# A Fourier layer and two expert layers on one core: ScalarE's order in the expert steps, and eight more conversion turns in the transform

## The chip, the cores and the metric

The kernel runs as one program on one core of a Trainium2 chip. The metric is the device time of that program in microseconds (us). Three runs of the kernel before gave 1172.59, 1174.08 and 1174.28 us; the median is 1174.08 us.

## The reference

Three layers follow each other on 2 x 3008 tokens of 256 numbers:

```
X = rfft(x, axis=1);  Yr = Xr @ w_r - Xi @ w_i + b_r;  Yi = Xr @ w_i + Xi @ w_r + b_i
Y = sign(Y) * max(|Y| - 0.01, 0)          # on the real and the imaginary part
x1 = irfft(Y, n=3008)                      # 6016 x 256
h = x1 @ w_in;  x2 = (h * cos(h)) @ w_out  # w_in 256 x 2048, w_out 2048 x 256
h = x2 @ w_in2; out = (h * clip(h + 3, 0, 6) / 6) @ w_out2
```

The expert weights arrive as float64 and are turned into float32 on the core.

## The kernel before, in words

**Two float32r pieces.** Each operand of a matmul is split into a high part (a copy on ScalarE) and a low part (a subtraction on GpSimd or VectorE), and a product is three matmuls (`three`, L844).

**Transform.** The Fourier layer runs in 24 steps (`k2_step`, L711), one for each pair of frequencies of one batch: w products (`w_mm`, PSUM tile pp), their split (`w_split`, tiles ph), the second transform stage (`b_mm`, bp), the shrinkage (`shrink_a` on ScalarE, `shrink_b` on VectorE, `shrink_hi` on ScalarE, `shrink_lo` on VectorE, which writes sl), the first inverse stage (`v_mm`, vp) and its store to DRAM (`v_store`, u_dram). The last inverse stage works on 16 groups of columns with two slices each (`y_mm`, PSUM tile yp; `y_out` copies it out on ScalarE, to st or yo). Groups 0, 1 and 2 follow steps 15, 16 and 17 (L785); their operands u_sb and tg_sb are loaded by `load_u`, the first one after step 14 (L783), each next one by `y_out` of the second slice. Three transform blocks and the other 26 slices run in the expert part.

**Expert steps.** The loop at L966 has 96 steps k (48 for each expert layer; 8 to each block of tokens). A step computes seven products of a fast 2 x 2 block scheme in four PSUM banks a, b, c, d (tiles ha to hd); bank a is always bank 0. Each of the four results then goes through `first` (ScalarE, then VectorE), `second` (Sin on ScalarE and a VectorE product, first layer alone) and `split` (gh on ScalarE, gl on GpSimd), and is multiplied with w_out some steps later (`out_mm`, six matmuls, tile acc). In each of the steps 1 to 12 two slices of the inverse transform are done as well, both in bank 0: the first by `y_begin(); y_end()` (L1025), the second by `y_begin()` at L1030 and `y_end()` at L1036. So the second slice waits for the copy yo of the first one, and block a of the next step waits for the copy yo of the second one. `advance` (L931) takes one step further in building the tokens of the next block (tile tok: a copy on ScalarE, subtractions on GpSimd); in steps 4 to 7 it does so three times a step.

**Conversion turns.** `Converter` (L281) turns the float64 weights into float32 pieces beside all that. Its work is cut into turns; `cv.step(n)` does n of them. A chunk of weights (128 x 512) is loaded by SP (rawi, rawo), its magnitude is taken on ScalarE (`magnitude`, L200: one ACTIVATE, tiles cvai and cvao), and then five turns do `clamp`, `shift`, `top`, `exponent`, `rest`, one VectorE instruction each (L203, L206, L209, L212, L215); `rest` hands an addition to GpSimd, and every second chunk of w_in has two more turns of sums on GpSimd. While a chunk is in its five turns, the pieces of the chunk before it are cut on ScalarE (L275), subtracted on GpSimd (L173) and stored by SP (L255). The magnitude of the next chunk is put on a list by `rest` and is done at the next `catch_up()`: at the start of each turn (L350), twice in a transform step (L734, L739) and once in an expert step (L1022).

`RATE_W` (L49) gives the turns of a transform step at its three places, for steps 0 to 7, 8 to 15, 16 to 20, and 21 to 23. An expert step has turns at three places (`other`, L939): one before `ba.first()`, and up to step 5 two before `bd.first()` and two at the end; in steps 8 to 47 the middle place has none.

**What sets the order.** In the transform the orders of TensorE, ScalarE and SP are those of the program; VectorE and GpSimd are ordered by a planner, which starts a conversion instruction early when its operands are there. In the expert steps all five orders are those of the program. Each engine and SP's queue take their instructions in order, so one that waits holds up those behind it.

Of the kernel before, what the change touches and what calls it, by code (L numbers as in the profile page):

```python
# [45 lines left out]


LASTC = 20
RATE_W = ((2, 1, 2), (1, 0, 1), (1, 1, 1), (0, 0, 0))  # L49
XB = 3  # L50
STAGED = [0] * 9 + [1, 2, 4, 5, 7, 8, 10] + [12] * 10
Y_EARLY = range(15, 18)
# [71 lines left out]
def fourier_moe_moe_kernel(ctx, tc, x, w_r, w_i, b_r, b_i, ta, tg, fg, win1, wout1, win2, wout2, out):  # L124
# [42 lines left out]
    def pool_now():  # L167
        while later:
            op, tiles = later.pop(0)
            op(*tiles)  # L170
# [110 lines left out]
    class Converter:  # L281
# [10 lines left out]
        def add(self, m, cs):  # L292
            for c in cs:
                self.queue += [("i", m, c, 0), ("i", m, c, 1), ("o", m, c, 0), ("o", m, c, 1)]
            while len(self.loaded) < 2 - self.busy and self.queue:
                self.load()
# [14 lines left out]
        def chunk(self):  # L311
            first = self.prev[0][0] if self.prev else None
            tail = self.tail()
            if self.loaded:
                key, ops = self.loaded.pop(0)
                self.busy = 1
                if not self.begun:
                    for _ in range(3):
                        next(tail, None)
                        yield  # L320
                    ops["magnitude"]()
                for part in ("clamp", "shift", "top", "exponent", "rest"):
                    if first == "i" or part in ("top", "exponent", "rest"):
                        next(tail, None)
                    if part == "rest":
                        for _ in tail:
                            pass
                        pool_now()
                    ops[part]()
                    if part == "rest":  # L330
                        if self.loaded:
                            self.ahead.append(self.loaded[0][1]["magnitude"])
                    yield
                self.begun = bool(self.loaded)
                yield from ops["sums"]()
                if ops["split"]:
                    self.prev = (key, ops)
                self.busy = 0
                self.load()
            else:  # L340
                yield from tail
# [5 lines left out]
        def step(self, n):  # L347
            for _ in range(n):
                pool_now()
                self.catch_up()  # L350
                while next(self.course, "end") == "end":
                    if not self.loaded and not self.prev:
                        return
                    if self.prev and self.prev[0] == self.hold:
                        return
                    self.course = self.chunk()
# [6 lines left out]
    cv = Converter()  # L363
# [33 lines left out]
    def y_out(g, ec):  # L397
        yp, at = yp_t.pop((g, ec)), g * YT
        if 0 not in staged:
            staged[0] = persist.tile([128, 2, 2, 512], F32, tag="st", bufs=1, name="st0")  # L400
        for t in range(2):
            t0, t1 = max(at, t * HALF[0]), min(at + YT, (t + 1) * HALF[0])
            if t0 < t1:
                act.activation(staged[0][:, ec, t, t0 - t * HALF[0] : t1 - t * HALF[0]], yp[:, t0 - at : t1 - at], AF.Copy)
        first = max(STARTS[1] - at, 0)
        if first < YT:
            yo = persist.tile([128, 512], F32, tag="o", bufs=3, name=f"yo{g}_{ec}")
            act.activation(yo[:, first:YT], yp[:, first:YT], AF.Copy)  # L408
        if ec == 1:
            load_u(g + 1)  # L410
        for p in range(1, NJ):
            t0, t1 = max(at, STARTS[p]), min(at + YT, STARTS[p + 1])
            if t0 < t1:
                sp.dma_start(x_dram[0][p][ec, :, t0 - STARTS[p] : t1 - STARTS[p]], yo[:, t0 - at : t1 - at])
# [69 lines left out]
    with ExitStack() as actx:  # L484
        apool = actx.enter_context(tc.tile_pool(name="apool", bufs=1))
        with tc.manual_schedule(engines={mybir.EngineType.PE, mybir.EngineType.SP, mybir.EngineType.Activation}):
# [224 lines left out]
            def k2_step(i):  # L711
                now, late, last = (divmod(i - k, NP) for k in range(1, 4))
                b, p = divmod(i, NP)
                rate = RATE_W[i // 8 + (i > LASTC)]
                more = i < NB * NP
# [85 lines left out]
    with tc.manual_schedule(engines=engines):  # L801
# [39 lines left out]
        def bank(z, name):  # L841
            return psum.tile([128, 512], F32, tag=f"h{z}", bufs=1, name=name)

        def three(h, ws, xs, start, stop, n):  # L844
            for j, (w, x) in enumerate(((ws[0], xs[0]), (ws[0], xs[1]), (ws[1], xs[0]))):
                pe.matmul(h[:, :n], lhsT=w, rhs=x, start=start and j == 0, stop=stop and j == 2, skip_group_check=True)  # L846

        def weights(k, slot):
            m, q = k // G, k % STEPS
            w, i = wi_sb[m, q // 2], q % 2  # L850
            return [w[:, z, slot - SLOTS[m][0], i * 128 : (i + 1) * 128] for z in range(2)]

        def tokens(k, slot):
            jj = k // STEPS
            return [tok[jj][:, z, slot - SLOTS[k // G][0], : HALF[jj % NJ]] for z in range(2)]
# [66 lines left out]
        def prepare(k):  # L922
            nonlocal ready
            jj, q = divmod(k, STEPS)
            if jj + 1 == 2 * NJ:
                return
            if q == (1 if jj else 3):
                stage_in(jj + 1)
                ready = operands(jj + 1)

        def advance(k, spare):  # L931
            if k % STEPS > (1 if k >= STEPS else 3) and not (spare and k >= STEPS):
                next(ready, None)

        def drained(k):
            if k < 2 and pend:
                pend.pop(0)()
# [13 lines left out]
        def y_end():  # L951
            if y_open:
                y_out(*y_open.pop())
# [4 lines left out]
        def flush():  # L958
            while ended:
                finish(*ended.pop(0))  # L960

        def out_next(least=1):
            if len(waiting) >= least:
                out_mm(waiting.pop(0))

        for k in range(2 * G):  # L966
            n = HALF[k // STEPS % NJ]
            a, b, c, d = (bank(z, f"h{r}_{k}") for z, r in zip((0, 1, 2, 3) if k % 2 == 0 else (0, 3, 2, 1), "abcd"))
            ba, bd, be, bc = (Block(k, f, t, h) for f, t, h in ((0, 0, a), (0, 1, d), (1, 0, b), (1, 1, c)))

            def mm(h, w, x, start=False):
                three(h, weights(k, w), tokens(k, x), start, True, n)

            if k == 0:
                for h in (b, d):
                    pe.matmul(h, lhsT=weights(k, A11)[0], rhs=tokens(k, B11)[0], start=True, stop=True)
            mm(a, A11, B11, True)
            act.activation(b[:, :n], a[:, :n], AF.Copy)  # L978
            if old:
                od, oe, oc = old  # L980
                od.split()
                oe.second()
            drained(k)
            out_next(5)
            mm(c, S1, T1, True)
            p5 = persist.tile([128, 512], F32, tag="r", bufs=5, name=f"p5_{k}")
            act.activation(p5[:, :n], c[:, :n], AF.Copy)  # L987
            if old:
                oc.split()
            drained(k)  # L990
            mm(b, S2, T2)
            add(d, p5, b, n)
            if k == 0:
                drained(k)
                next(ready)
            flush()
            mm(a, A12, B21)
            if old:
                oe.split()
            prepare(k)  # L1000
            advance(k, False)
            defer[0] = 2
            other(k, 0)
            defer[0] = 1
            ba.first()
            if k == 0:
                drained(k)
            out_next()
            pool_now()
            mm(b, S3, T3)  # L1010
            add(c, p5, b, n)
            ba.second()
            if k == 0:
                next(ready, None)
            mm(d, S4, B22)
            if k == 0:
                drained(k)
            other(k, 1)
            bd.first()
            advance(k, True)  # L1020
            bc.first()
            cv.catch_up()  # L1022
            out_next()
            if k:
                y_begin()  # L1025
                y_end()
            bd.second()
            mm(b, A22, T4)
            if k:
                y_begin()  # L1030
            else:
                drained(k)
            be.first()
            advance(k, False)
            bc.second()
            y_end()  # L1036
            out_next()
            other(k, 2)
            ba.split()
            flush()  # L1040
            old = bd, be, bc
            waiting += [ba, bd, be, bc]
            w_loads(k)
# [50 lines left out]
```

## Time and profile before

| | |
|---|---|
| median of three runs | 1174.08 us |
| profiled execution: its own time | 1174.28 us |
| its span, first to last instruction | 1172.5 us |
| TensorE busy | 1153.6 us (98%) |
| VectorE, ScalarE, GpSimd busy | 767.0, 811.3, 807.6 us |
| granted TensorE clock, mean | 0.998 |

Matmuls overlap, so busy time is a union of their spans, and short holes between two starts can hide in it. A wait of TensorE is best read from the timeline: the idle time in brackets, and the distance of two starts.

### The profile page before, as it was taken

What the parts mean: (1) busy time and instruction counts of PE and PEld (TensorE: products, weight loads), DVE (VectorE), ACT (ScalarE), POOL (GpSimd) and SP (SyncE); (2) the same over time, 40 slices, a digit from 0 to 9 for tenths busy, and PEclk for the clock granted to TensorE, in tenths of its full rate; (3) what the DMA queues carried; (4) which work ended last, traced back from release to release, by engine and by line L of the source; (5) the groups of instructions that cost most, each with busy time, mean ns of one, the idle gap of its engine ahead of it and who ended that gap; (6) DMA issues with size and microseconds to landing.
All of it is one profiled execution on the core that took longest, in us unless ns stands there. A gap on an engine that the chain in (4) does not pass through costs nothing.

```text
span 1172.5 us, 15903 instructions
## 1 busy us (share of the span) xinstructions
PE 1153.6 (98%) x5363; PEld 966.2 (82%) x5363; DVE 767.0 (65%) x1098; ACT 811.3 (69%) x1546; POOL 807.6 (69%) x654
## 2 busy tenths in 40 slices
PE   8999999999999999999999999999999999999998
PEld 7887877778888888888889987888888888888897
DVE  5888778786679888988897677643343444433442
ACT  4677677777788888888788875565566556556554
POOL 3566536896787797888887786557757667577544
PEclk9999999999999999999999999999999999999999
DMA  8646639635413113104115420020020010100000
GB/s 214 183 124 180 180 88 292 218 100 163 144 54 104 41 59 131 37 18 149 36 37 180 182 93 1 1 72 1 1 72 1 19 54 1 67 1 1 37 1 32
DMA packets 48106, 98.71 MB, mean 84 GB/s; under 512 B 6228, under 2 KB 22840, under 8 KB 47384
## 3 DMA queue, kind: packets, MB, share of 16 engines
q1 hardware_dynamic: 47768, 97.54, 26.2%
q8 instruction: 42, 0.69, 0.2%
q14 instruction: 40, 0.33, 0.1%
q10 hardware_dynamic: 256, 0.15, 0.0%
HBM read 59.53 MB, written 38.14 MB: 83 GB/s over the span
## 4 chain that ended last, share of the span: by engine, by line
PE 88%; DMA 3%; DVE 3%; ACT 2%; issue 2%; POOL 2%; POOLq 0%; ACTq 0%; SPq 0%; DVEq 0%
PE acc L846 41%; PE hb L846 15%; PE ha L846 11%; PE hc L846 5%; PE hd L846 5%; PE pp L633 4%; PE bp L660 2%; PE yp L389 2%; PE zp L528 1%; POOL gl L173 1%; PE vp L699 1%; DMA ta_big<-in_ta_dram 1%; DMA x_big<-in_x_dram 1%; DVE r L822 0%; DMA tg_sb<-in_tg_dram 0%
## 5 line engine op out<-in xcount | busy, mean ns | idle before, releaser
L173 POOL TENSOR_TENSOR gl<-r,gh 128x512 fp32r<-128x512 f32 (+1 forms) x384 | 501.3, 1321 | 280.7 <-ACT gh L837 264.4
L846 PE MATMUL acc<-gh,wo 128*128 128x512 f32 (+1 forms) x1536 | 529.6, 386 | 0.0
L846 PEld LDWEIGHTS acc<-gh,wo 128*128 128x128 f32 x1536 | 288.4, 188 | 53.5
L846 PE MATMUL acc<-gl,wo 128*128 128x512 f32 (+1 forms) x768 | 296.0, 385 | 0.6 <-POOL gl L173 0.6
L846 PE MATMUL hb<-tok,wi 128*128 128x512 f32 (+1 forms) x864 | 241.0, 387 | 0.6 <-DVE hc L858 0.6
L837 ACT ACTIVATE gh<-r 128x512 fp32r<-128x512 f32 (+1 forms) x384 | 227.6, 615 | 0.4 <-PE acc L846 0.4
L846 PEld LDWEIGHTS hb<-tok,wi 128*128 128x128 f32 x864 | 161.0, 188 | 31.1 <-DVE hc L858 2.0
L858 DVE TENSOR_TENSOR hd<-p,hb 128x512 f32<-128x512 f32 (+1 forms) x96 | 65.8, 685 | 164.1 <-PE hb L846 159.1
L846 PEld LDWEIGHTS acc<-gl,wo 128*128 128x128 f32 x768 | 144.2, 188 | 27.6 <-POOL gl L173 1.0
L846 PE MATMUL ha<-tok,wi 128*128 128x512 f32 (+1 forms) x576 | 160.5, 387 | 2.5 <-ACT yo L408 2.5
L830 ACT ACTIVATE r<-r 128x512 f32<-128x512 f32 (+1 forms) x192 | 118.9, 619 | 57.9 <-DVE r L822 57.9
L846 PEld LDWEIGHTS ha<-tok,wi 128*128 128x128 f32 x576 | 107.5, 188 | 24.8 <-ACT yo L408 5.1
L447 POOL TENSOR_TENSOR tok<-st,tok 128x512 fp32r<-128x512 f32 (+1 forms) x77 | 97.6, 1283 | 2.9 <-ACT tok L444 2.9
L987 ACT ACTIVATE p<-hc 128x512 f32<-128x512 f32 (+1 forms) x96 | 56.5, 588 | 58.2 <-PE hc L846 58.2
L824 ACT ACTIVATE r<-hd 128x512 f32<-128x512 f32 (+1 forms) x48 | 28.3, 589 | 78.1 <-PE hd L846 78.1
L846 PE MATMUL hc<-tok,wi 128*128 128x512 f32 (+1 forms) x288 | 80.2, 387 | 1.1 <-DVE r L831 1.1
L978 ACT ACTIVATE hb<-ha 128x512 f32<-128x512 f32 (+1 forms) x96 | 55.2, 575 | 37.7 <-PE ha L846 37.5
L846 PE MATMUL hd<-tok,wi 128*128 128x512 f32 (+1 forms) x288 | 79.7, 385 | 0.0
L858 DVE TENSOR_TENSOR hc<-p,hb 128x512 f32<-128x512 f32 (+1 forms) x96 | 65.4, 681 | 15.7 <-PE hb L846 14.9
L846 PEld LDWEIGHTS hc<-tok,wi 128*128 128x128 f32 x288 | 53.8, 188 | 12.5 <-DVE r L831 2.6
L846 PEld LDWEIGHTS hd<-tok,wi 128*128 128x128 f32 x288 | 54.1, 188 | 10.1
L450 POOL TENSOR_TENSOR st<-st 128x512 f32<-128x512 f32 (+1 forms) x44 | 57.9, 1317 | 1.2
(141 smaller groups left out, 1681.0 us busy)
## 6 DMA issues: line engine op xcount, KB each, us to landing
st<-x_dram SPq DMA_DIRECT2D x18, 512.0 KB, 4.7
wi<-wi_dram SPq DMA_DIRECT2D x5, 1792.0 KB, 8.3
rawi<-in_win_dram SPq DMA_DIRECT2D x16, 512.0 KB, 3.9
rawo<-in_wout_dram SPq DMA_DIRECT2D x16, 512.0 KB, 4.0
u_dram<-v SPq DMA_DIRECT2D x48, 128.0 KB, 2.4
u_sb<-u_dram SPq DMA_DIRECT2D x16, 384.0 KB, 3.9
wo<-wo_dram SPq DMA_DIRECT2D x10, 512.0 KB, 6.9
x_dram<-o SPq DMA_DIRECT2D x20, 256.0 KB, 2.2
```

The source lines that it names most:

```text
L173: nc.gpsimd.tensor_tensor(out, x, y, op=ALU.subtract)
L389: pe.matmul(yp[:, i * TP : (i + 1) * TP], lhsT=u_sb[g][:, i, ec * 128 : (ec + 1) * 128], rhs=tg_sb[g][:, i * TP : (i + 1) * TP], start=Tru ...
L447: subtract(at(lo, t), src, f32(at(hi, t)), op=ALU.subtract)
L450: subtract(z, x, y, op=ALU.subtract)
L633: pe.matmul(pp.rearrange("p a e -> p (a e)"), lhsT=za[:, p, kc, 2 * (k2 % 2) : 2 * (k2 % 2) + 2, :].rearrange("p r n -> p (r n)"), rhs=wb[ ...
L824: act.activation(r, h, AF.Relu, bias=3.0, scale=1.0)
L830: act.activation(r, r, AF.Sin, bias=math.pi / 2, scale=1.0)
L837: act.activation(gh[:, :n], self.r[:, :n], AF.Copy)
L846: pe.matmul(h[:, :n], lhsT=w, rhs=x, start=start and j == 0, stop=stop and j == 2, skip_group_check=True)
L858: dve.tensor_tensor(h[:, :n], r[:, :n], x[:, :n], op=ALU.add)
L978: act.activation(b[:, :n], a[:, :n], AF.Copy)
L987: act.activation(p5[:, :n], c[:, :n], AF.Copy)
```

## The change

Four edits:

1. `RATE_W`: one turn at the middle place of transform steps 8 to 15, where there was none: eight more turns in all, so that every later turn comes earlier, until the converter stops at its hold.
2. The start of a turn no longer catches up; a magnitude still on the list is done by the `clamp` turn, behind the piece that this turn cuts.
3. In the expert step `catch_up()` moves from behind `bc.first()` to behind `bc.second()`.
4. `y_end()` of the second slice moves ahead of `advance(k, False)` and `bc.second()`, directly behind `be.first()`.

```diff
-RATE_W = ((2, 1, 2), (1, 0, 1), (1, 1, 1), (0, 0, 0))
+RATE_W = ((2, 1, 2), (1, 1, 1), (1, 1, 1), (0, 0, 0))
...
-                    if part == "rest":
+                    if part == "clamp":
+                        self.catch_up()
+                    elif part == "rest":
                         for _ in tail:
                             pass
                         pool_now()
...
                 pool_now()
-                self.catch_up()
                 while next(self.course, "end") == "end":
...
             bc.first()
-            cv.catch_up()
             out_next()
             if k:
                 y_begin()
...
             be.first()
+            y_end()
             advance(k, False)
             bc.second()
-            y_end()
+            cv.catch_up()
             out_next()
```

## Rows read from the trace of the kernel before

**Rows 1.** The page: busy us (share) xinstructions.

```profile
PE 1153.6 (98%) x5363; PEld 966.2 (82%) x5363; DVE 767.0 (65%) x1098; ACT 811.3 (69%) x1546; POOL 807.6 (69%) x654
```

**Rows 2.** Waits of PE, whole span: line waited for, us in total, times, longest.

```profile
PE ha L846 <- ACT yo L408: 2.5, 4, 1.3
PE yp L389 <- ACT yo L408: 1.5, 4, 0.5
PE vp L699 <- DVE sl L693: 1.3, 2, 1.0
PE yp L389 <- DVE r L831: 0.9, 2, 0.4
```

**Rows 3.** Stretches: length, busy PE (x) PEld DVE ACT POOL, PEclk, DMA, GB/s.

```profile
77.00:117.00 40.00, 38.38 (x175) 31.69 (x174) 33.20 (x46) 31.58 (x61) 27.83 (x22) 1.00 0.59 173
116.70:120.10 3.40, 3.40 (x15) 3.02 (x14) 3.30 (x6) 1.46 (x3) 1.12 (x2) 0.50 0.40 116
183.00:305.00 122.00, 117.45 (x581) 95.24 (x580) 93.17 (x130) 93.81 (x181) 90.42 (x73) 1.00 0.56 178
305.00:1148.00 843.00, 842.39 (x3790) 707.94 (x3790) 526.60 (x748) 587.34 (x1111) 611.14 (x483) 1.00 0.16 54
```

**Rows 4.** Timeline of PE: start us, us, instruction [idle before <-releaser]; waits of transform and steps.

```profile
115.71 2.83 PE L389 MATMUL yp<-tg_sb,u_sb 96*128 96x94 f32 x16 [1.62 <-DMA tg_sb<-in_tg_dram]
130.58 0.69 PE L389 MATMUL yp<-tg_sb,u_sb 96*128 96x94 f32 x5
...
148.05 0.39 PE L699 MATMUL vp<-sh,fgr 128*128 128x512 f32 x1
149.47 0.50 PE L699 MATMUL vp<-sl,fgr 128*128 128x512 f32 x1 [1.03 <-DVE sl L693]
...
185.37 1.13 PE L389 MATMUL yp<-tg_sb,u_sb 96*128 96x94 f32 x8 [0.37 <-ACT yo L408]
188.14 0.96 PE L846 MATMUL ha<-tok,wi 128*128 128x512 f32 x3 [0.23 <-ACT yo L408]
...
227.57 0.97 PE L846 MATMUL ha<-tok,wi 128*128 128x512 f32 x3 [0.73 <-ACT yo L408]
241.32 0.96 PE L846 MATMUL ha<-tok,wi 128*128 128x512 f32 x3 [1.32 <-ACT yo L408]
```

**Rows 5.** Timeline of ACT, expert steps 1 and 5: same columns.

```profile
183.29 0.70 ACT L200 ACTIVATE cvai<-rawi 128x512 f32<-128x512 f32 x1 [1.17 <-POOL whio020l L173]
...
238.49 0.58 ACT L821 ACTIVATE r<-hb 128x512 int32<-128x512 f32 x1
239.75 0.63 ACT L444 ACTIVATE tok<-st 128x512 fp32r<-128x512 f32 x1 [0.68 <-POOL st L450]
240.28 0.61 ACT L830 ACTIVATE r<-r 128x512 f32<-128x512 f32 x1
240.80 0.46 ACT L408 ACTIVATE yo<-yp 128x376 f32<-128x376 f32 x1
```

**Rows 6.** Timeline of DVE in transform steps 10 and 20, same columns.

```profile
89.16 0.42 DVE L203 TENSOR_SCALAR cvao<-cvao 128x512 f32<-128x512 f32 x1
...
143.23 1.28 DVE L203 TENSOR_SCALAR cvao<-cvao 128x512 f32<-128x512 f32 x1
144.54 1.40 DVE L206 TENSOR_SCALAR cvao<-cvao 128x512 uint32<-128x512 uint32 x1
145.86 0.68 DVE L683 SCALAR_TENSOR_TENSOR u<-bp,u 128x512 f32<-128x512 f32 x1
147.66 1.76 DVE L693 TENSOR_TENSOR sl<-u,sh 128x512 fp32r<-128x512 f32 x1
```

**Rows 7.** Timeline of POOL beside the second row of rows 6, same columns.

```profile
142.94 1.29 POOL L447 TENSOR_TENSOR tok<-st,tok 128x512 fp32r<-128x512 f32 x1
```

**Rows 8.** Timeline of SP's queue (issue of DMAs), same columns.

```profile
126.35 0.37 SPq L380 DMA_DIRECT2D tg_sb<-in_tg_dram  x1
```

**Rows 9.** The page's DMA issues: KB each, median us from issue to landing.

```profile
u_sb<-u_dram SPq DMA_DIRECT2D x16, 384.0 KB, 3.9
```

## The prediction

> **What bounds the kernel now.** I read the page first: TensorE is busy 1153.6 of 1172.5 us, and no other engine reaches 70% [rows 1]. Then the stretches: from 305 to 1148 us TensorE is busy 842.39 of 843 us, and its 3790 matmuls come one every 0.22 us [rows 3]. Nothing can be won there, and something is lost only where another engine would become late by whole microseconds. So the time is the matmuls plus the holes ahead of 305 us and at the two ends, and the third view is TensorE's own waits [rows 2]. Of these the change can touch four kinds: block a of the next step waits for the copy yo of the second slice (2.5 us, 4 times), a slice waits for yo of the one before (1.5 us, 4 times, one of them in the drain) or for VectorE to free bank 0 (0.9 us, twice), and v_mm waits for sl (1.3 us, twice). The largest single hole, 1.62 us at 115.71, is the first slice of group 0 waiting for its load [rows 4], and behind it the clock is granted at 0.50, which is 1.2 of 2.4 GHz, for 3.4 us [rows 3].
>
> A wait costs more than its idle time shows, because the pipeline has to fill again: at 149.47 the idle time is 1.03 us, but the two starts lie 149.47 - 148.05 = 1.42 us apart where 0.22 is usual, so 1.20 us are lost [rows 4]. I add 0.17 us to each wait.
>
> **Part 1: the second slice's copy (edit 4).** It adds no instruction. In step 5 ScalarE does the block's first copy at 238.49, then stands 0.68 us for a token copy that waits for GpSimd, then does the Sin and only at 240.80 the copy yo [rows 5]; block a starts at 241.32 after 1.32 us of idle time [rows 4]. With yo directly behind the first copy, it starts at 238.49 + 0.58 = 239.07 at the latest, 1.7 us earlier; that is more than the wait, which goes: 1.32 + 0.17 = 1.5 us. In step 4 only the Sin is jumped (0.61 us by its row in step 5, some 0.5 us when overlapped with its neighbour), against a wait of 0.73 us; about 0.55 of its 0.90 us goes. In step 1 the 0.5 us cover the 0.23 us: 0.4 us gone. The fourth wait (2.5 - 1.32 - 0.73 - 0.23, so 0.2 us, in step 2) I count as 0.25 us, since that step gets more ScalarE work ahead of the copy (part 2). Sum 2.7 us, bounds 1.5 (step 5 alone) and 2.5 + 4 x 0.17 = 3.2 us.
>
> What is late next: the Sin of `bc.second()` moves behind yo by one copy, 0.47 us [rows 5], and so does the VectorE product that frees bank c for the next step. TensorE asks for it only after block a and six `out_mm` matmuls, nine matmuls or 2.0 us after block a begins; that covers 0.5 us. The moved token copy of `advance` comes 0.47 us later too, and its readers belong to the next block of tokens. The same copy also lets SP's store of yo and the load of the next group (L410) leave earlier; that costs nothing.
>
> **Part 2: magnitudes (edits 2 and 3) and where the turns now fall.** Counting the code's turns, the converter of the first weights has 91, and before the change 67 are done when the transform ends; afterwards it is 75. So in expert step 1 stand turns 76 to 80 instead of 68 to 72, and so on. In step 1 a magnitude stood ahead of `bd.first()`: 0.70 us, and 1.17 us of waiting for GpSimd to release its buffer [rows 5]. It is gone from there, since its chunk is now converted in the transform; the second slice then no longer waits (0.37 us [rows 4]) and 0.54 us are won. In step 2 two cuts and a magnitude (three instructions of about 0.6 us) take the place of the magnitude and a like wait: nothing won. Step 3 keeps a magnitude at that place. Step 4 has one magnitude there instead of two cuts, and no cut ahead of `ba.first()`, which should take most of one of the two VectorE waits of 0.44 us [rows 2]: 0.5 us. Step 6 loses a cut, 0.2 us. Against this stand 0.2 us for new small waits in steps 2, 5 and 7. Sum 1.0 us won; bounds: all of (1.5 - 0.5 + 0.9) + 5 x 0.17 = 2.8 us won, and as much lost, because the same queues get other work. I take the value near the row of step 1, the only one whose cause is wholly removed.
>
> The later magnitudes (edit 3 in steps 13 to 95) move within a stretch in which TensorE stands 0.6 us of 843 [rows 3]: zero.
>
> **Part 3: eight more turns in steps 8 to 15 (edit 1).** They hold the five VectorE instructions of one chunk, the clamp of the next, two turns of sums for GpSimd, one cut and two magnitudes. All this work existed and leaves the expert steps, so only its place counts. VectorE is busy 33.2 of 40 us in these steps [rows 3]. Six more instructions are 3 x 0.42 + 0.43 + 2 x 0.68, so 3.1 us, by the undisturbed rows, and 6 x 1.40, so 8.4 us, by the slow ones [rows 6]; I take 4 us, near the undisturbed ones, since a chunk rarely has more than one or two slow instructions. VectorE then stands at 37 of 40, and sl and ph, which TensorE reads a step (4.8 us) later, should stay in time mostly. Cost: 0.4 us, bounds -0.5 and 5.
>
> Two waits here move. At 147 us, clamp (1.28) and shift (1.40) ran ahead of u and sl, and TensorE lost 1.20 us [rows 4, 6]. Afterwards that step has only one clamp to do late, and the piece subtractions of the chunk before it lie earlier; I count half, 0.6 us won (bounds 1.2 won, 1.2 lost). And SP's order in step 16 now has the stores of four pieces (two turns) ahead of the load of group 2. Its second part was issued at 126.35, and such a load lands after 3.9 us [rows 8, 9], at 130.25, where the slice starts at 130.58 [rows 4]: 0.3 us of slack, which stores in flight will eat. Cost 0.4 us, bounds 0 and 3.3 (the hole of 115.71: 1.62 idle and 1.7 for 3.4 us at half clock). The wait at 115.71 itself stays: v_store of step 14 is gated as before, since a magnitude still falls into step 13, and no store stands between it and the load.
>
> The Trainium skill ("SBUF — State Buffer", section "Who interferes with whom") says that a VectorE instruction with two SBUF inputs, or in a two-port mode, locks out GpSimd or is locked out for a whole instruction. The trace agrees in one place: the same clamp took 0.42 us at 89.16 and 1.28 us at 143.23, where a GpSimd subtraction was running from 142.94 to 144.23 [rows 6, 7]. By that rule the eight turns cost the high bound of 8.4 us on VectorE; the sum above goes by the rows near the low one.
>
> **Sum.** Won 2.7 + 1.0 + 0.6, lost 0.4 + 0.4: 3.5 us. The profiled execution took 1174.28 us, 1.8 us of it outside the span, and lies 0.2 us above the median. 1174.08 - 3.5 = 1170.6 us.
>
> **The rivals.**
> A, the gain goes to the next in line (no change): the copies come earlier, but the wait passes to VectorE's r of block d, which sits behind conversion instructions of 1.3 to 1.4 us [rows 6] and gates bd's Sin ahead of `be.first()`. Then only step 5 pays (1.5 us), and the transform's new waits take 0.8: 1174.08 - 0.7 = 1173.4 us. For it: in step 5 ScalarE waited for an engine, not for its own queue [rows 5]. Against: steps 1 and 4 are short by less than one Sin.
> B, slower: VectorE's backlog in steps 8 to 20. If every chunk's five instructions run slow, sl comes late as at 149.47, 1.20 us each time, for the six chunks that then fall into steps 8 to 20 instead of once. It decides from the point where VectorE's work there passes 40 us: 33.2 + 8.4 = 41.6 us does. Price 5 x 1.20 = 6.0 us more, and 3.3 us more if the load of group 2 falls behind the stores and the clock drops again: against the 4.3 us won this gives 1176 to 1179, middle 1177.5 us. For it: the slow rows. Against: from 77 to 117 us VectorE worked 83% and TensorE waited for it nowhere; its waits in these steps were DMA's.
> C, faster still: the wait at 115.71 shrinks, because v_store of step 14 comes earlier, and the clock stays full. The wait at 241.32, 1.32 us, lies in a stretch granted 1.00 [rows 3, 4], so a slightly shorter hole may do. Worth up to 1.62 + 1.7 = 3.3 us: 1167.3 us. Against: nothing in the change aims at it.
> D, it does not do what it says: the planner, which already starts conversions early, leaves VectorE's order in the transform as it was. Magnitudes on ScalarE gate these instructions and do move, so this can hold only in part; then parts 1 and 2 remain: 1170.8 us, counted with the forecast.
>
> **How the numbers follow.** A measurement of this kernel tells 0.2% (2.3 us) from no change, so faster is below 1171.7, slower above 1176.4 us. Forecast with D 0.56 (1168.8 to 1172.3 alone; some 0.1 of it above 1171.7), A 0.22, B 0.13, C 0.09. Faster 0.46 + 0.09 and 0.02 of A: 0.57. Slower: most of B, 0.12. Same: 0.31. The range leaves out the ends of B and C: 1167.0 to 1176.5 us.
>
> **What would show it.** Right: in TensorE's waits the row of block a for yo is gone or below 0.5 us; in step 1 no magnitude stands ahead of `bd.first()`; in the timeline of ScalarE yo follows the copy of hb at once; the row of the load at 115.71 stands at 1.3 to 1.9 us with 3.4 us at 0.50 behind it. Wrong: rows of vp for sl, or of bp or pp, above 2 us in all between 77 and 162 us; a wait for tg_sb at group 2; new waits of TensorE between 305 and 1148 us.

## The result, and the profile after

The changed kernel is slower: 1187.19 us (median of 4 runs, 1184.21 to 1189.77) against 1173.47 us for the kernel before on the same chip. The ratio is 1.0110, with a 95% interval from 1.0094 to 1.0126. That is clear of the noise, and above the forecast of 1170.6 us and the upper end of its range, 1176.5 us.

The page of the changed kernel, first part, in the columns of [rows 1]; its span is 1183.4 us, its own time 1185.23 us:

```profile
PE 1159.9 (98%) x5363; PEld 968.9 (82%) x5363; DVE 775.3 (66%) x1098; ACT 811.7 (69%) x1546; POOL 810.8 (69%) x654
```

The work is the same to the instruction; VectorE's instructions took 8.3 us longer. TensorE's waits over the whole span, as in [rows 2] (their line numbers are one higher than before):

```profile
PE vp L700 <- DVE sl L694: 4.4, 4, 1.7
PE yp L390 <- DVE r L832: 3.2, 4, 2.0
PE yp L390 <- DMA tg_sb<-in_tg_dram: 3.1, 3, 1.9
PE vp L700 <- ACT sh L689: 1.9, 2, 1.8
...
PE bp L661 <- DVE ph L648: 0.8, 1, 0.8
```

The waits of block a for yo (2.5 us) are gone, as forecast. In their place stand sl, sh and ph, which are transform operands, and VectorE's r. The stretches, as in [rows 3]:

```profile
77.00:117.00 40.00, 36.49 (x157) 28.56 (x155) 36.73 (x48) 28.26 (x56) 29.84 (x23) 1.00 0.60 182
...
148.70:155.60 6.90, 5.32 (x13) 4.22 (x14) 6.54 (x8) 4.69 (x9) 5.37 (x5) 0.51 0.29 68
295.40:302.40 7.00, 7.00 (x24) 5.94 (x24) 3.93 (x5) 3.12 (x6) 1.28 (x1) 0.51 0.70 243
305.00:1148.00 843.00, 841.96 (x3788) 706.31 (x3787) 521.08 (x746) 587.66 (x1112) 604.33 (x477) 1.00 0.15 52
```

In steps 8 to 15 VectorE is busy 36.73 us instead of 33.20, and TensorE 36.49 instead of 38.38. Two stretches of about 7 us run at half clock, where the kernel before had one of 3.4 us. From 305 to 1148 us next to nothing is lost, as before.

Where the time went is seen best by when the same matmul starts in both traces. The table gives the start in the changed kernel minus the start before; 1.73 us that the execution after gained ahead of the first w product are taken out. A `b_mm` is named by the pair of frequencies it works on; the program does it at the end of the next step (that of pair 18 ends step 19).

| matmul | difference, us | what lies in between |
|---|---|---|
| `b_mm` of pair 10 | +0.08 | |
| `b_mm` of pair 14 | +4.26 | three late operands (ph, sl, sl): 0.91, 1.40 and 1.32 us lost |
| `b_mm` of pair 15 | +2.96 | load of group 0: its hole stays, no half clock behind it |
| `b_mm` of pair 18 | +4.59 | loads of groups 1 and 2: 0.53 and 0.96 us lost |
| `b_mm` of pair 19 | +10.25 | sh and sl late, half clock |
| block a of expert step 0 | +9.75 | the old wait at 149.47 is gone, half clock runs on until 155.5 |
| block a of step 6 | +6.90 | gain in the expert steps: 2.85 us |
| block a of step 9 | +7.59 | |
| block a of step 10 | +12.23 | a wait of 1.96 us, half clock |
| block a of step 95 | +12.66 | |

So two places cost 5.66 us (pair 18 to 19) and 4.64 us (expert step 9 to 10), the pairs 10 to 14 cost 4.18 us and the loads of groups 1 and 2 cost 1.63 us: 16.1 us in all. Against this stand 2.85 us won in the expert steps, 0.50 us at the old wait, and 1.30 us at group 0's load, where the clock did not fall.

**Step 19 of the transform.** This is the work for pair 17, which TensorE reads between the `b_mm` of pairs 18 and 19; the old wait at 149.47 was one step later, for sl of pair 18. VectorE's timeline; a bracket is idle time and its releaser:

```profile
140.84 1.36 DVE L203 TENSOR_SCALAR cvai<-cvai 128x512 f32<-128x512 f32 x1
142.23 1.39 DVE L206 TENSOR_SCALAR cvai<-cvai 128x512 uint32<-128x512 uint32 x1
143.66 1.67 DVE L209 SCALAR_TENSOR_TENSOR cvai<-rawi,cvai 128x512 uint32<-128x512 uint32 x1
145.36 1.39 DVE L212 TENSOR_SCALAR cvbi<-cvai 128x512 uint32<-128x512 uint32 x1
146.67 0.68 DVE L684 SCALAR_TENSOR_TENSOR u<-bp,u 128x512 f32<-128x512 f32 x1
...
148.47 1.75 DVE L694 TENSOR_TENSOR sl<-u,sh 128x512 fp32r<-128x512 f32 x1
```

Four conversion instructions stand in a row ahead of u and take 5.81 us. The operand of u was there when ScalarE's `shrink_a` ended, at 142.07 us; u started 4.6 us later. GpSimd's timeline beside it shows token subtractions without a gap:

```profile
140.62 2.72 POOL L448 TENSOR_TENSOR tok<-st,tok 128x512 fp32r<-128x512 f32 x2 [2.22 <-ACT tok L445]
143.30 1.48 POOL L451 TENSOR_TENSOR st<-st 128x512 f32<-128x512 f32 x1
144.74 1.73 POOL L448 TENSOR_TENSOR tok<-st,tok 128x512 fp32r<-128x512 f32 x1
146.43 4.92 POOL L451 TENSOR_TENSOR st<-st 128x512 f32<-128x512 f32 x3
```

And TensorE's timeline: two holes, then matmuls at a distance of 0.42 us where 0.22 is usual.

```profile
148.07 0.49 PE L700 MATMUL vp<-sh,fgr 128*128 128x512 f32 x1 [1.75 <-ACT sh L689]
150.28 0.80 PE L700 MATMUL vp<-sl,fgr 128*128 128x512 f32 x1 [1.72 <-DVE sl L694]
150.87 0.63 PE L700 MATMUL vp<-sh,fgr 128*128 128x512 f32 x1
151.29 0.63 PE L634 MATMUL pp<-wh,zh 128*128 128x512 f32 x1
```

**The pairs 10 to 14.** The same pattern in short: clamp (1.52 us, from 93.95 us on) and shift are slow beside GpSimd's subtractions, top behind them is not, and ph, which TensorE reads at 97.55 us, stands behind the slow two. GpSimd's row and VectorE's:

```profile
93.43 3.19 POOL L173 TENSOR_TENSOR zl<-z,zh 128x512 fp32r<-128x512 f32 x2
```

```profile
95.50 1.40 DVE L206 TENSOR_SCALAR cvai<-cvai 128x512 uint32<-128x512 uint32 x1
96.82 0.68 DVE L648 TENSOR_TENSOR ph<-pp,ph 128x512 fp32r<-128x512 f32 x1
97.42 0.67 DVE L209 SCALAR_TENSOR_TENSOR cvai<-rawi,cvai 128x512 uint32<-128x512 uint32 x1
```

Two slow instructions of 1.51 and 1.40 us stand ahead of the third hole too, from 105.38 us on, beside subtractions from 103.61 to 108.03 us. That they are slow because of GpSimd is read from these rows alone; no kernel here took GpSimd's work away at that place.

**Expert step 9.** SP's queue first. Four stores of wi pieces, which fell elsewhere before, stand ahead of the stores of o:

```profile
285.31 0.42 SPq L255 DMA_DIRECT2D wi_dram<-whii101h  x1
285.83 0.40 SPq L255 DMA_DIRECT2D wi_dram<-w  x1
286.28 0.81 SPq L255 DMA_DIRECT2D wi_dram<-whii101h  x1
287.18 0.63 SPq L255 DMA_DIRECT2D wi_dram<-w  x1
287.90 3.92 SPq L883 DMA_DIRECT2D x_dram<-o  x4
```

VectorE's copy of the next o waits for a buffer that these stores release, and r, which TensorE needs, is queued behind it (VectorE's timeline):

```profile
290.79 0.69 DVE L882 COPY o<-acc 128x512 f32<-128x512 f32 x1 [2.02 <-DMA x_dram<-o]
291.39 1.26 DVE L203 TENSOR_SCALAR cvao<-cvao 128x512 f32<-128x512 f32 x1
292.57 0.68 DVE L823 SCALAR_TENSOR_TENSOR r<-r,ha 128x512 f32<-128x512 int32 x1
```

In TensorE's timeline the slice behind it starts late by about as much:

```profile
294.69 1.32 PE L390 MATMUL yp<-tg_sb,u_sb 96*128 96x94 f32 x8 [1.96 <-DVE r L832]
```

### The profile page after: what moved, and what is told of

Read it like the earlier page. It is cut to its first block, busy times and chain, and to the rows that moved or that the text cites. A ratio compares the mean times of both kernels' runs of the same rounds, so it can differ in the third digit from the quotient of the medians.

```text
span 1183.4 us, 15916 instructions
## 1 busy us (share of the span) xinstructions
PE 1159.9 (98%) x5363; PEld 968.9 (82%) x5363; DVE 775.3 (66%) x1098; ACT 811.7 (69%) x1546; POOL 810.8 (69%) x654
## 4 chain that ended last, share of the span: by engine, by line
PE 78%; DVE 5%; issue 5%; POOL 4%; DMA 4%; ACT 2%; SPq 1%; POOLq 0%; DVEq 0%; ACTq 0%
PE acc L847 38%; PE hb L847 15%; PE ha L847 10%; PE hc L847 5%; PE hd L847 5%; POOL gl L173 3%; PE yp L390 2%; PE pp L634 2%; DMA tg_sb<-in_tg_dram 1%; PE bp L661 1%; DMA ta_big<-in_ta_dram 1%; PE zp L529 1%; DMA x_big<-in_x_dram 1%; DVE u L684 0%; DVE cvai L209 0%
## 5 line engine op out<-in xcount | busy, mean ns | idle before, releaser
L832 DVE TENSOR_TENSOR r<-r,hb 128x512 f32<-128x512 f32 (+1 forms) x48 | 32.3, 674 | 40.0 <-ACT r L831 39.7
```

The source lines that it names most:

```text
L832: dve.tensor_tensor(r, r, self.h[:, : self.n], op=ALU.mult)
```

## The experiments

Every kernel ran beside the kernel before on its own chip, so the ratios compare best. Two kernels ran once; of these I read the traces alone. "Whole" is the changed kernel.

| kernel | median us (runs) | before | ratio, 95% interval |
|---|---|---|---|
| edit 1 alone | 1183.40 (4) | 1173.55 | 1.0073 (1.0052 to 1.0094) |
| edits 2 to 4 | 1172.59 (10) | 1173.55 | 0.9987 (0.9977 to 0.9996) |
| edit 4 alone | 1174.60 (10) | 1173.55 | 1.0004 (0.9994 to 1.0015) |
| edits 2 and 3 | 1171.62 (8) | 1173.55 | 0.9983 (0.9970 to 0.9995) |
| the same again | 1171.58 (11) | 1173.22 | 0.9988 (0.9979 to 0.9997) |
| whole, tokens later | 1181.88 (1) | 1172.83 | |
| whole, four o buffers | 1182.93 (1) | 1172.83 | |
| whole, both of these | 1176.55 (6) | 1173.22 | 1.0028 (1.0017 to 1.0040) |
| whole, first tokens left out | 1181.28 (6) | 1172.69 | 1.0071 (1.0050 to 1.0093) |
| whole, turns in steps 0 to 7 | 1189.69 (4) | 1172.83 | 1.0134 (1.0111 to 1.0158) |
| edits 2 to 4, tokens on VectorE | 1173.69 (10) | 1172.83 | 1.0008 (0.9998 to 1.0018) |
| edits 2 to 4, tokens behind yo | 1171.19 (11) | 1173.22 | 0.9981 (0.9973 to 0.9990) |

**Which edit costs.** Edit 1 alone, then edits 2 to 4 without it.

```diff
-RATE_W = ((2, 1, 2), (1, 0, 1), (1, 1, 1), (0, 0, 0))
+RATE_W = ((2, 1, 2), (1, 1, 1), (1, 1, 1), (0, 0, 0))
```

> Edit 1 alone (eight more turns in transform steps 8 to 15; magnitudes and the slice's copy as before). Theory T1: the loss is edit 1's own, through VectorE's queue in the transform and SP's queue at expert step 9. Then expert step 0 begins 8 to 12 us later against the first pp matmul than before, step 9 to 10 loses 3 to 5 us, none of the 3 us of the expert steps is won, and the time is 1184 to 1191 us. Rival T2: the loss comes from the magnitudes' new places (edits 2 and 3), which bunch the conversion instructions; then this kernel stays below 1177 us.

> Edits 2, 3 and 4 without the eight turns. T1: the transform costs what it did (expert step 0 within 1 us of before, counted from the first pp matmul), step 9 shows no wait above 0.5 us, the waits of block a for yo are gone, and the time is 2 to 4 us below before: 1169.5 to 1171.5 us. T2: 1178 us or more, with VectorE late in the transform.

Edit 1 alone gives a ratio of 1.0073. Its trace shows holes at the same places: the three between pairs 10 and 14 (0.85, 1.39 and 1.33 us lost), sl in step 19 (1.98 us lost), and the slice in expert step 9 (2.12 us lost). Edits 2 to 4 without the turns are a little faster than the kernel before, and have none of these holes. So the eight turns are the cause, T1, and T2 falls. The sizes were off: edit 1 alone is at 1183.40 us, just below the 1184 expected, expert step 0 starts 7.6 us later instead of 8 to 12, and from step 0 to step 6 it wins 1.47 us where nothing was expected; edits 2 to 4 are 1.0 us below the kernel before by the medians, where 2 to 4 were expected.

Together the edits are worse than edit 1 alone, by 3.8 us of the medians. By estimate the half clock makes up 2.4 us of it: span times (1 - granted clock) is 7.7 us at the median clock of the whole change's runs and 5.3 us at that of edit 1's, each known to about 1 us. In the two traces 3.0 us stand in one place, from pair 18 to 19: edit 1 alone loses 2.63 us there, and the clock stays full. VectorE and GpSimd have the same order there in both, but not the same times. In edit 1 alone the token copies on ScalarE stood behind a magnitude that waited 1.13 us for its raw weights, and GpSimd's token subtractions began at 143.38 us. Clamp and shift (142.81 and 143.28 us) took 0.43 us each, top and exponent behind them 1.66 and 1.40: two slow instructions instead of four. Why the clock fell behind the one and not behind the other stays open.

**Edit 4, and edits 2 and 3, by themselves.** Edit 4 alone:

```diff
             be.first()
+            y_end()
             advance(k, False)
             bc.second()
-            y_end()
```

> Edit 4 alone (the second slice's copy ahead of advance and bc.second). T1: the wait of block a for yo falls from 2.5 us to below 0.5 us, everything ahead of step 1 is as before, and the time is 2 to 3.5 us below before: 1170 to 1171.5 us. If the wait only passes to another releaser, within 1 us of before.

> Edits 2 and 3 alone (magnitudes at the clamp turn and behind bc.second; y_end as before). T1: within 1.5 us of before, 1172 to 1175 us, with the transform unchanged. T2: most of the loss of the whole change is here, 1180 us or more.

> Edits 2 and 3 once more, without the copy's move and without the eight turns, to see whether the gain of the first measurement (ratio 0.9983, interval 0.9970 to 0.9995) holds. If it does: ratio 0.997 to 0.9995 again and a time 1 to 3 us below the kernel before. If that was the clock's spread between executions: ratio within 0.9995 to 1.001.

The gain expected of edit 4 is not in its time (ratio 1.0004). Its trace shows why: block a gains 1.97 us from step 1 to step 6 on the kernel before, and gives 3.74 us back by step 8. Half clock from 251.8 us on, for 3.41 us, is part of that. The giving back begins in ScalarE's timeline of step 6:

```profile
246.13 0.58 ACT L821 ACTIVATE r<-hd 128x512 int32<-128x512 f32 x1
248.58 0.63 ACT L444 ACTIVATE tok<-st 128x512 fp32r<-128x512 f32 x1 [1.87 <-POOL st L450]
249.12 0.58 ACT L821 ACTIVATE r<-hc 128x512 int32<-128x512 f32 x1
249.60 0.48 ACT L408 ACTIVATE yo<-yp 128x376 f32<-128x376 f32 x1
```

The first slice's yo stands behind a token copy (`advance(k, True)`) that waits 1.87 us for GpSimd, and the second slice, which waits for yo, loses 1.59 us at 250.13. In the kernel before GpSimd was busy 36.67 us of the 40 from 215 to 255 us:

```profile
215.00:255.00 40.00, 37.06 (x182) 29.58 (x181) 30.99 (x44) 31.67 (x62) 36.67 (x29) 1.00 0.44 134
```

So steps that become shorter seem to meet GpSimd as the next bound. Edits 2 and 3 alone keep their gain, 1.4 to 2 us by the intervals' middles, twice measured; the first time 1171.62 us lay just below the expected 1172 to 1175, the second agrees with what was expected. In both traces some 0.65 us of it is the wait at 149.47 [rows 4], which shrinks from 1.20 to 0.55 us. Another 1.7 us stands in the first trace alone, where no half clock followed group 0's load.

**A way round GpSimd.** First the second block's token subtractions on VectorE, then the token copies behind the first slice's yo.

```diff
-        subtract = (dve if jj == NJ + 1 else nc.gpsimd).tensor_tensor
+        subtract = (dve if jj in (1, NJ + 1) else nc.gpsimd).tensor_tensor
```

```diff
             bd.first()
-            advance(k, True)
             bc.first()
             out_next()
             if k:
                 y_begin()
...
                 y_end()
+            advance(k, True)
```

> Edits 2 to 4 without the eight turns, and the token subtractions of block 1 (expert steps 4 to 7) on VectorE instead of GpSimd. Theory G: edit 4's 2.7 us are given back in step 6 because GpSimd is the bound in steps 4 to 6 (36 of 40 us busy) and a token copy on ScalarE waits for it ahead of bc.first; with that work moved, block a of step 7 stays 4 us or more ahead of before and the time is 1 to 3 us below edits 2 to 4: 1169.5 to 1171.5 us. Rival V: VectorE takes over as the bound; 1172 us or more.

> Edits 2 to 4 without the eight turns, and the second slice's token copies of a block stand behind the first slice's y eviction in ScalarE's order, no longer ahead of its last transform. Theory G (in steps 4 to 6 the earlier token copy waits for GpSimd's stores and holds up the first slice's transforms and yo): the wait of 1.6 us at yp in step 6 falls below 0.5 us, acc waits stay near 1 us, and the time is 1 to 2.5 us below that of edits 2 to 4 together (1172.6), so 1170 to 1171.8 where the kernel before is at 1174. Rival V2 (GpSimd has no slack in steps 4 to 6 and whatever stands behind it is late wherever the copy stands): the start of step 7 against the kernel before stays within 0.6 us of where edits 2 to 4 left it (-2.3), and the time within 0.6 us of 1172.6.

The first way failed: block a gains nothing from step 1 to step 6 and loses 2.1 us from there to step 8. VectorE is busy 40.08 of 45 us from 215 to 260 us (34.47 in the kernel before), and GpSimd 31.36, as rival V has it:

```profile
215.00:260.00 45.00, 42.43 (x203) 33.28 (x202) 40.08 (x54) 36.06 (x71) 31.36 (x24) 1.00 0.45 137
```

That VectorE alone holds TensorE up is not shown: from 205 to 270 us TensorE waits 1.4 us for VectorE's r, but also 1.5 us for GpSimd's gl. The time of this trace, 1177.06 us, is the highest of its ten runs.

The second way worked in its place. In ScalarE's timeline of step 6 `bc.first()` (hc) follows `bd.first()` (hd) at once, and the token copy stands behind yo and waits for nothing:

```profile
247.17 0.58 ACT L822 ACTIVATE r<-hd 128x512 int32<-128x512 f32 x1
247.65 0.59 ACT L822 ACTIVATE r<-hc 128x512 int32<-128x512 f32 x1
249.07 0.48 ACT L409 ACTIVATE yo<-yp 128x376 f32<-128x376 f32 x1 [0.83 <-PE yp L390]
249.63 0.63 ACT L445 ACTIVATE tok<-st 128x512 fp32r<-128x512 f32 x1
```

The longest wait of a slice for yo falls from 1.4 to 0.5 us, and from step 6 to step 7 only 0.66 us are given back instead of 2.66. Theory G holds by these rows. Step 7 starts 2.2 us before that of the kernel before, where V2 had it too, but the trace of edits 2 to 4 came into step 0 with 3.0 us in hand, this one with 1.0: from step 0 to 7 the first gives back 0.73 us and this one wins 1.19. By the medians the gain over edits 2 to 4 is 1.4 us, by the ratios 0.7 us, with intervals that overlap. At 0.9981 this is the fastest kernel measured here, beside edits 2 and 3 alone.

**Step 19: what made VectorE slow.** First the tokens some steps later; then a kernel in which they stand where they were and GpSimd reads nearly nothing: it leaves out most of the subtractions, so its first block of tokens is not that of the reference.

```diff
-OPERANDS = (2, 2, 2, 2, 1, 1)
+OPERANDS = (0, 0, 2, 2, 3, 3)
```

```diff
+        few = (slice(None), slice(0, 16))
         def low(t, src):
+            if jj == 0:
+                nc.gpsimd.memset(f32(at(lo, t)), 0.0)
+                return
...
         def less(z, x, y):
+            if jj == 0:
+                z, x, y = z[few], x[few], y[few]
```

> The changed kernel with the token subtractions of block 0 moved from transform steps 18 and 19 to steps 20 to 23 (OPERANDS 0, 0, 2, 2, 3, 3 instead of 2, 2, 2, 2, 1, 1; the same number of turns). Theory P: in step 19 the conversion instructions are slow (1.36 to 1.67 us each) because GpSimd's subtractions run beside them; without these they take 0.4 to 0.7 us, u of step 19 is less than 2.5 us late (4.6 before), and the last bp of step 19 falls from 5.7 us lost to below 2 us. Rival Q: four conversion instructions in a row ahead of u cost the same wherever GpSimd works; then step 19 still loses over 4 us.

> The whole change, with VectorE's order exactly as in it, but the token subtractions of the first block of tokens on GpSimd (those beside transform steps 18 and 19) are left out: four of them are cut to 16 of 512 columns, the others are replaced by a fill with zero that reads nothing; so the tokens of the first block are not those of the reference. Theory (GpSimd's subtractions make the four conversion instructions ahead of u slow, and that is what costs step 19): clamp, shift, top and exponent take 0.4 to 0.7 us each instead of 1.36 to 1.67, u starts some 3.9 us earlier, the loss of 5.7 us in step 19 falls below 1.5 us, and the time lies 4 to 6 us below the whole change, at 1181 to 1183. Rival (the order is enough: four instructions that the planner puts ahead of u make it late whatever runs beside them): TensorE still waits 2 us or more for sh and sl there, and the time stays at 1185 or above.

With the tokens later, the 5.66 us of step 19 fall to 0.00: `b_mm` of pair 18 and of pair 19 both start 6.75 us after those of the kernel before. But the planner had also put u ahead of `top` and `exponent` there, so that the run did not tell speed from order. In the second kernel VectorE's order is that of the whole change. Its timeline (line numbers seven higher from L445 on):

```profile
144.00 0.42 DVE L203 TENSOR_SCALAR cvai<-cvai 128x512 f32<-128x512 f32 x1
144.45 0.43 DVE L206 TENSOR_SCALAR cvai<-cvai 128x512 uint32<-128x512 uint32 x1
144.91 0.74 DVE L209 SCALAR_TENSOR_TENSOR cvai<-rawi,cvai 128x512 uint32<-128x512 uint32 x1
145.69 0.43 DVE L212 TENSOR_SCALAR cvbi<-cvai 128x512 uint32<-128x512 uint32 x1
146.03 0.68 DVE L691 SCALAR_TENSOR_TENSOR u<-bp,u 128x512 f32<-128x512 f32 x1
```

The same four take 2.02 us instead of 5.81, TensorE waits nowhere from 144 to 154 us, and both `b_mm`, of pair 18 and 19, start 6.02 us after those before: the loss of the step is 0.00 us. The rival, that the order is enough, falls. GpSimd's subtractions beside them made the four slow, and that was the whole of step 19; edit 1 alone, with the same order and two slow instructions, lies between. The median, 1181.28 us, is in the expected range; the runs spread from 1175.98 to 1183.56 us.

**Expert step 9: a fourth o buffer.** A wi buffer makes room for it.

```diff
-                return persist.tile([128, 2, 256], F32R, tag="whi", bufs=4, name=f"whi{name}{z}")
+                return persist.tile([128, 2, 256], F32R, tag="whi", bufs=3, name=f"whi{name}{z}")
...
-                o = persist.tile([128, 512], F32, tag="o", bufs=3, name=f"o{jj}_{t}{d}")
+                o = persist.tile([128, 512], F32, tag="o", bufs=4, name=f"o{jj}_{t}{d}")
```

> The changed kernel with four buffers for tile o instead of three (and, to make room, three for the cut pieces whi instead of four). Theory S: the 4.6 us of expert step 9 come from VectorE's copy of an accumulator, which waits 2.0 us for a buffer of o whose store stands behind four stores of pieces on SP's queue; with a fourth buffer that wait goes and block a of step 10 starts within 1.5 us of before, counted from block a of step 9. Rival R: the magnitude and the clamp ahead of ba.first do it; then step 9 still loses over 2 us.

> The whole change with both remedies in one kernel: second slice's token copies of the transform two turns later, and four o buffers with three wi buffers. Theory (the two holes, step 19 of the transform and step 9 of the expert pass, are what costs): both are gone, about 4.5 and 4 us of them, and with the half clock behind them the time falls by 7 to 10 us against the whole change, to 1177 to 1180. Rival (VectorE's load in the transform comes back at another step, and the load of the second group's wi meets another buffer): one of the losses reappears elsewhere and the time stays at 1182 or above.

With it the same copy of acc waits for no buffer (VectorE's timeline; the clamp behind it waits for its magnitude and is slow, and r still comes late by 0.87 us):

```profile
292.32 0.68 DVE L882 COPY o<-acc 128x512 f32<-128x512 f32 x1
293.69 1.37 DVE L203 TENSOR_SCALAR cvao<-cvao 128x512 f32<-128x512 f32 x1 [0.69 <-ACT cvao L200]
```

From step 9 to 10 the loss is 0.77 us instead of 4.64, while step 19 still loses 6.07. So the wait is that of the buffers behind SP's stores. Both remedies in one kernel give 1176.55 us, 10.6 us below the whole change by the medians, slightly below the expected 1177 to 1180; in its trace pairs 18 to 19 lose 0.00 us and expert step 9 loses 0.78. The kernel is still 3.3 us above the kernel before by both medians. Its trace loses 5.45 us from pair 9 to pair 14 (1.33 of it ahead of pair 10, where the whole change lost 0.08) and 0.80 us at the loads behind them.

**Steps 8 to 15: the turns elsewhere.** The eight turns in steps 0 to 7, where TensorE had no hole before.

```diff
-RATE_W = ((2, 1, 2), (1, 1, 1), (1, 1, 1), (0, 0, 0))
+RATE_W = ((2, 2, 2), (1, 0, 1), (1, 1, 1), (0, 0, 0))
```

> The changed kernel with its eight extra turns in steps 0 to 7 (2, 2, 2) and steps 8 to 15 at (1, 0, 1) as before: from step 16 on every turn stands where it stands in the changed kernel. Theory L: the losses in steps 11 to 14 (some 4 us) belong to the load in steps 8 to 15 and go; those in steps 16 to 19 and in expert step 9 belong to where the turns then fall and stay: 1181 to 1185 us. Rival: all of the loss is load in steps 8 to 15; then below 1177 us.

Pairs 8 to 14 then lose 0.29 us instead of about 4.2, so it is the turns' place that costs there; step 19 (5.86 us) and expert step 9 (4.58 us) lose as before, since from step 16 on every turn lies where the whole change has it. The time, 1189.69 us, is a miss: it lies above the expected 1181 to 1185. Up to pair 8 it loses 9.6 us, 6.8 of them around one hole of TensorE at 35.53 us, 4.39 us of idle time. ScalarE's timeline ahead of it:

```profile
33.30 0.66 ACT L200 ACTIVATE cvai<-rawi 128x512 f32<-128x512 f32 x1 [6.14 <-DMA rawi<-in_win_dram]
33.86 0.58 ACT L647 ACTIVATE ph<-pp 128x512 fp32r<-128x512 f32 x1
```

A magnitude, pulled ahead by a turn, waits 6.14 us for its raw weights, with ph behind it in the queue.

## Why the prediction was wrong, point by point

**What bounds the kernel.** Right: nothing was lost after 305 us, and every loss stands in holes ahead of it.

**Part 1, the copy.** The mechanism is right: block a no longer waits for yo. Parts 1 and 2 together won 2.85 us from step 0 to step 6, where 3.7 were forecast; edit 4 alone won 1.97 of its 2.7 up to there, and edit 1 alone, by the shifted turns, 1.47. But what is late next was named wrongly. I looked at the Sin and at VectorE's product; in edit 4 alone it was the token copy that waits for GpSimd, and nothing was left. Rival A had the gain pass to the next in line, but put it on VectorE's r.

**Part 2, where the turns fall.** That the later magnitudes cost zero held from step 13 on. But the sum follows the shifted turns through steps 1 to 7 alone and puts steps 8 to 12 at nothing without a reason. In step 9 the shift costs 4.64 us, by SP's stores and three o buffers. I had followed the shifted turns on ScalarE alone, although the same text follows SP's stores in step 16.

**Part 3, the eight turns: the step that failed.** The load on VectorE was sized well: 4 us were forecast, 36.73 - 33.20, so 3.5 us, came. What failed is the sentence that sl and ph "should stay in time mostly", at 0.4 us: pairs 10 to 14 lose 4.18 us, inside the bound of 5. It was argued from a mean load, and a mean doesn't show a row of instructions ahead of one that TensorE waits for. The same sentence failed worse in step 19. The term for the wait at 147 us looked at step 20 alone, and there it held: that wait is gone, 0.6 us were forecast, 0.50 came and 1.33 where the clock stayed full (first tokens left out). But four conversion instructions moved one step ahead, for which the sum has no term. All four were slow, and with the half clock they lose 5.66 us; that a chunk "rarely has more than one or two slow instructions" is refuted by the timeline itself. The load of group 2 lost 0.96 us, 0.4 were forecast; that of group 1 lost 0.53, none were. The hole at group 0's load stayed, but the clock did not fall behind it, which gave 1.3 us: luck for the forecast, which had no such term; rival C had priced it, for a shorter hole.

In all 16.1 us were lost where the sum has 0.8, and some 4.7 us won where it has 4.3.

**The rivals.** B had the right mechanism and the wrong point from which it decides. It asked for VectorE above 40 us in the stretch; it took effect at 36.73. It also priced each late sl at the 1.20 us of [rows 4], while a run of slow instructions cost two holes of 1.92 and 1.98 us and a clock that fell behind them. The row of the slow clamp and the Trainium skill ("SBUF — State Buffer", section "Who interferes with whom") both spoke for it. By that section a VectorE instruction in a two-port mode, or with two SBUF inputs, and a GpSimd instruction that reads SBUF shut each other out. The trace agrees: with most of GpSimd's reads taken away, the four instructions take 2.02 us instead of 5.81.

## What to carry to other kernels

Before a shared order is moved, write down what then stands directly ahead of each instruction that the bounding engine waits for, and price that row of instructions at its slow durations if another engine works beside it; the mean load of a stretch does not show it. When all later turns shift, follow every queue they issue to: a store that moves ahead of another holds back the buffer which that one releases. When a step gets shorter, look for the engine that is nearest to full in it.

## What the runs showed of the hardware

A hole of TensorE has two prices. The slice in expert step 9 lost 2.12 us at its start in the whole change and in the kernel without the first tokens alike. In the first the clock was granted at 0.51 behind it, its lower level of 1.2 GHz, and the step cost 4.64 us; in the second it stayed at 1.00, 2.4 GHz, and the step cost 2.02 us. The stretch in the second kernel (slice at 292.77 us):

```profile
290.00:300.00 10.00, 8.04 (x43) 6.48 (x42) 7.82 (x11) 6.46 (x13) 2.75 (x3) 1.00 0.82 276
```

Which of the two follows differed from trace to trace at one and the same hole: behind group 0's load it was half clock before [rows 3] and full clock in the whole change, although the hole there was longer (1.90 us of idle time, against 1.62). With edits 2 and 3 alone the two traces of the same kernel differ in this, and their starts behind it by 1.7 us. What decides it these runs do not show.
